# First loads over two queues, whole x tiles, a full-height gate matmul, and an order laid out anew

## The chip, the cores and the metric

One core of a Trainium2 chip runs the kernel. The metric is device time in microseconds of one execution. Its engines work beside each other and meet only at semaphores: TensorE (PE, with its weight loads shown as PEld), VectorE (DVE), ScalarE (ACT), GpSimd (POOL) and SyncE (SP), which here only issues DMAs.

## What is computed

The input x is 2048 tokens of 512 numbers in bf16. Two branches work on it, and a gate of one number for each token mixes them:

```python
g = sigmoid((x * gate_w).sum(-1, keepdims=True))
a = A(x)   # 32 heads of 16; 4 segments of 512 tokens: causal softmax inside a segment,
           # plus a linear memory (phi(q) M / phi(q) z) of the segments before; then @ wo
b = B(x)   # h = relu(x @ W_gate) * (x @ W_up), 1792 wide; then h @ W_down
out = g * a + (1 - g) * b
```

The row `gate_w` has 512 numbers. The kernel needs it on all 128 partitions, so that VectorE can multiply a tile of 128 tokens by it and sum along the row.

## The kernel before

**Stages.** The tokens are worked in four segments of 512. For each segment TensorE makes q and k (transposed, line 788) and v (by tokens, line 786) from x transposed, then visits attention 18 times: a visit (line 908, helper `visit`) computes scores of four heads at once, each head in 32 rows of the array. ScalarE takes the exponential of a visit (line 924), GpSimd masks its diagonal (line 930), and TensorE multiplies by v in packed form (line 964). The feed-forward branch runs beside it: gate and up matmuls (line 1038), relu on ScalarE or VectorE (lines 1046, 1047), the product on VectorE (line 1049), and for each segment the down matmuls (line 1077) and the output projection (line 1070) into one bank. The accumulated memory of the keys is line 831, its use line 851.

**The order.** No loop order is fixed. `program` describes every instruction as an `Op` with the engines that can do it, an estimate of its time, what it reads and writes, and a queue with a priority. `Sched.run` then places one op after the other, by the estimated times, on five engines and 16 DMA semaphores, and writes each engine's instruction list with the waits that it needs. Each engine then runs its list strictly in that order. The planner adds `SWITCH` (line 28) where TensorE changes between kinds of matmul, has a DMA land by a formula in `place` (line 405), and a list of seeds (line 546), one for each 8 us of planned time, that shifts priorities and breaks ties (`knob`, `jitter`). Changing one of these can move every later instruction. `after` on an op is the earliest planned time of its start: 6400 ns for the gate row's matmul, 12000 ns for the first visit.

**The start.** Before anything else can run, x must be transposed for segment 0. `load` puts loads on the list of SP or of ACT (line 598). Before, SP issues four x tiles (into `hT`), four tiles of wq, four of wk, four of wv, the small `braw`, then four half-width tiles of W_gate (`wg`), four of W_up (`wu`), and the second halves. ACT issues a tiny load of wq's corner and the gate row (into row 0 of `oTt`); later, between its other work, it issues tiny loads of the corners of W_gate, W_up and W_down, all into `adT`, so that each waits for the one before. TensorE runs filler matmuls on constants (line 670), transposes the x tiles against an identity that GpSimd has built (lines 647, 648; the matmuls are line 683), and DVE and ACT copy the results to `xT` (lines 693, 695). Tiles 0 and 1 are copied whole, tiles 2 and 3 in halves. Then come more filler matmuls (`warm1`, line 701), the first q matmuls, and the matmul that spreads the gate row over the partitions (line 704): its stationary operand is one row of ones, its moving operand row 0 of `oTt`. ACT copies that to `gwb` (line 706) and DVE multiplies and sums (line 734).

In the first part of q, three output tiles take the first, then the second tile of wq, and so on, so that a matmul can start as soon as its tile of wq is there. The copies out of PSUM are lines 793 (ACT) and 797, 801, 814 (DVE). At most two banks are held by projections at a time.

The places in the planner that the change touches:

```python
op.end = self.dma_busy + (1400.0 if start < 16000.0 else 5200.0 if start < 60000.0 else 3200.0)
...
xps.append(pe(lambda e: e.matmul(PL[:, 2, :], lhsT=nc.const_aps.tensor(1.0, [128, 128], BF16)[0:1, :], rhs=V.oTt[0:1, :], start=True, stop=True), 300, reads=["oTt"], writes=["bankL2"], name="gwx"))
```

Of the kernel before, what the change touches and what calls it, by code (L numbers as in the profile page):

```python
# [11 lines left out]
BF16 = mybir.dt.bfloat16  # L12
# [12 lines left out]
TNN = 4  # L25
STRICT = 6000.0
PE_LAT = 175.0
SWITCH = 100.0
GATE_T = {1: 44000.0, 2: 90000.0, 3: 140000.0}
UNIT_T = 400.0  # L30
NBLK = 36
# [91 lines left out]
class Sched:  # L123
# [240 lines left out]
    def place(self, op, e, start):  # L364
        op.eng = e
        if op.ep is not None and op.role == "w" and op.ep.bank is None:
            got = self._banks(op, e)[0]
            for ep, bi in zip([g[0] for g in got], sorted(g[1] for g in got) if op.ep.cls == "main" else [g[1] for g in got]):
                for i in range(bi, bi + ep.nb):
                    if self.bank_ep[i] is not None:  # L370
                        op.preds += [(r, False) for r in self.bank_ep[i].readers]
                    self.bank_ep[i] = ep
                ep.bank = bi
        if e == "pool" and self.yield_to is not None:
            op.preds.append((self.yield_to, False))
# [12 lines left out]
        if e == "pool":  # L388
            if start > self.now["pool"] + 1.0:
                self.pool_from = start  # L390
        if e == "pe":
            if op.mode != self.mode or start > self.now[e] + 60.0:
                occ += SWITCH
            self.mode = op.mode
        if op.dma:
            d = min(range(self.ndma), key=lambda i: (self.dma_end.get(i, 0.0), i))
            st = f"dma{d}"
            if self.cnt[st] > 0:
                self._waits(e, {st: self.cnt[st]})
            self.cnt[st] += 1  # L400
            self.semval[st, self.cnt[st]] = self.semval.get((st, self.cnt[st] - 1), 0) + 16 * op.nd
            inc = 16
            issued = start + occ
            self.dma_busy = max(self.dma_busy, issued) + op.nbytes / 340.0
            op.end = self.dma_busy + (1400.0 if start < 16000.0 else 5200.0 if start < 60000.0 else 3200.0)
            self.dma_end[d] = op.end
        else:
            st = e
            self.cnt[st] += 1
            inc = 1  # L410
            op.end = start + occ + op.lat
        idx = self.cnt[st]
        self.prog[e].append(("ins", op, st, inc))
        op.stream, op.idx, op.start, op.done = st, idx, start, True
        if op.mates:
            self.mates = op.mates
        if e == "pe" and op.ep is not None and op.ep.cls == "main":
            self.low_from = True
        sn = dict(self.know[e])
        sn[st] = max(sn[st], idx)  # L420
        self.snap[st][idx] = sn
        self.now[e] = start + occ
        self.busy[e] += occ
        self.log.append((start, start + occ, e, op.name))
# [115 lines left out]
def build_kernel(nc, A_x, A_wq, A_wk, A_wv, A_wo, A_beta, W_g, W_u, W_d, gate_w, out):  # L540
    _, S, D = A_x.shape
    F = W_g.shape[1]
    assert D == 512 and S % 512 == 0 and F % 128 == 0
    NSEG, KT, NF, NT = S // 512, D // 128, F // 128, S // 128
    EPS, SCALE = 1e-6, 16 ** -0.5
    sc = Sched(seeds=(140892, 575458, 0, 581332, 635069, 619273, 262375, 763595, 0, 238677, 585783, 19046, 187739, 0, 462444, 519459, 197962, 296149, 243870, 832001, 511906, 535245, 636171, 100007, 0, 121574, 418075, 0, 0, 346384, 0,))
    T = {}
    with contextlib.ExitStack() as stack:
        for name, shape, dt in plan(S, D, F):
            T[name] = stack.enter_context(nc.sbuf_tensor(name, shape, dt))  # L550
        PS = stack.enter_context(nc.psum_tensor("ps", [128, 8, 512], F32))
        for st in sc.streams:
            sc.sem[st] = stack.enter_context(nc.semaphore(f"s_{st}"))
        program(sc, nc, T, PS, A_x, A_wq, A_wk, A_wv, A_wo, A_beta, W_g, W_u, W_d, gate_w, out, NSEG, KT, NF, NT, EPS, SCALE)
        with nc.Block() as block:
            sc.emit(block)
    return sc


def program(sc, nc, T, PS, A_x, A_wq, A_wk, A_wv, A_wo, A_beta, W_g, W_u, W_d, gate_w, out, NSEG, KT, NF, NT, EPS, SCALE):  # L560
    V = type("V", (), T)
# [28 lines left out]
        return PS[:, ep.bank, :] if ep.nb == 1 else PS[:, ep.bank:ep.bank + 2, :]  # L590

    def xt(c):
        return [f"xT{c % XR}_{kt}" for kt in range(KT)] if c % XR else [f"xT0_{i}" for i in (range(6) if c == 0 else (0, 1, 2, 4))]

    lact, lsp = [], []

    def load(eng, names, dst, src, nbytes, occ=460.0):
        (lact if eng == "act" else lsp).append(dma(eng, lambda e, dst=dst, src=src: e.dma_start(dst, src), nbytes, occ=occ, writes=names, name="ld" + names[0]))  # L598
    x0 = A_x[0, 0:512, :].rearrange("(i p) d -> p i d", p=128)
    def touch(n, src):  # L600
        load("act", ["adT"], V.adT[0:16, 32 * n:32 * n + 32], src, 1024)
    touch(0, A_wq[0:16, 0:32])
    load("act", ["oTt"], V.oTt[0:1, :], gate_w.rearrange("(a n) -> a n", a=1), 1024)
    for i in range(4):
        load("sp", [f"hT{i}"], V.hT[:, i, :], x0[:, i, :], 1 << 17)
    for nm, w, src in (("wq", V.wq, A_wq), ("wk", V.wk, A_wk), ("wv", V.wv, A_wv)):
        for kt in range(KT):
            load("sp", [f"{nm}{kt}"], w[:, kt, :], src[kt * 128:(kt + 1) * 128, :], 1 << 17)
    half = (NF // 2) * 128
    hs_ = ((0, half), (half, NF * 128))  # L610

# [50 lines left out]
        ds.append(dve(lambda e, b=b: e.memset(PS[:, 4 + b, :], 0.0), 500, writes=[f"init{b}"], name=f"init{b}"))  # L662
    ds.append(dve(lambda e: e.reduce_sum(V.pm[:, :], V.pm8[:, :].rearrange("q (j p) -> q p j", p=2), AX.X), 180, reads=["pm8"], writes=["pm"], name="pm"))
    sc.queue(0, ds)
    sc.queue(1, st)

    def warm(m, n, k, b):
        def fn(e):
# [3 lines left out]
        return pe(fn, m * n * (0.834 if k == 0 else 0.5), writes=[f"bankL{b}"], name=f"warm{k}")  # L672

    xps, xcs = [warm(5, 512, 0, 3)], []
    for n, (i, k0, k1, bank, eng) in enumerate(((0, 0, 4, 0, "dve"), (1, 0, 4, 1, "act"), (2, 0, 2, 2, "dve"), (2, 2, 4, None, "act"), (3, 0, 2, 3, "dve"), (3, 2, 4, None, "act"))):
        ep = Epoch("att") if bank is None else None

        def B(ep=ep, bank=bank):
            return A(ep) if bank is None else PL[:, bank, :]

        def fx(e, i=i, k0=k0, k1=k1, B=B):
            for kt in range(k0, k1):
                ins = e.matmul(B()[:, kt * 128:(kt + 1) * 128], lhsT=V.hT[:, i, kt * 128:(kt + 1) * 128], rhs=V.ident[:], start=True, stop=True)  # L683
            return ins
        w = 128 * (k1 - k0)
        bk = [] if bank is None else [f"bankL{bank}"]
        xps.append(pe(fx, 108 * (k1 - k0), reads=[f"hT{i}", "ident"], writes=bk, name=f"xt{n}", ep=ep, role=None if ep is None else "w"))

        def src(B=B, k0=k0, k1=k1):
            return B()[:, k0 * 128:k1 * 128].rearrange("q (k t) -> q k t", t=128)  # L690
        dst = V.xT[:, k0:k1, i * 128:(i + 1) * 128]
        if eng == "dve":
            xcs.append(dve(lambda e, d=dst, src=src: e.tensor_copy(d, src()), t_dve(w), reads=bk, writes=[f"xT0_{n}"], name=f"xc{n}", ep=ep, role=None if ep is None else "r"))
        else:
            xcs.append(act(lambda e, d=dst, src=src: e.activation(d, src(), ACT.Copy), t_act(w), reads=bk, writes=[f"xT0_{n}"], name=f"xc{n}", ep=ep, role=None if ep is None else "r"))
# [1 line left out]
    epw = Epoch("att")  # L697

    def warm1(e):
        for n in (128, 128, 128, 128):  # L700
            ins = e.matmul(A(epw)[:, 0:n], lhsT=nc.const_aps.tensor(1.0, [128, 128], BF16), rhs=nc.const_aps.tensor(1.0, [128, n], BF16), start=True, stop=True)
        return ins
    xps.append(pe(warm1, 380, name="warm1", ep=epw, role="w"))
    xps.append(pe(lambda e: e.matmul(PL[:, 2, :], lhsT=nc.const_aps.tensor(1.0, [128, 128], BF16)[0:1, :], rhs=V.oTt[0:1, :], start=True, stop=True), 300, reads=["oTt"], writes=["bankL2"], name="gwx"))  # L704
    xps[-1].after = 6400.0
    xcs.append(act(lambda e: e.activation(V.gwb[:], PL[:, 2, :], ACT.Copy), t_act(512), reads=["bankL2"], writes=["gwb"], name="gwc"))
    sc.queue(0, xps)
# [66 lines left out]
    def proj(s):  # L774
# [3 lines left out]
        def pj(w, col, name, wname, tokmajor=False):  # L778
# [3 lines left out]
            for k0 in range(0, KT, step):  # L782
                def fn(e, k0=k0):
# [3 lines left out]
                        else:  # L787
                            ins = e.matmul(A(ep)[:, :], lhsT=w[:, kt, col * 128:(col + 1) * 128], rhs=V.xT[:, kt, tok:tok + 512], start=(kt == 0), stop=(kt == KT - 1))  # L788
                    return ins
                pes.append(pe(fn, mm(512, step), reads=[f"{wname}{kt}" for kt in range(k0, k0 + step)] + (xt(s) if not early or k0 > 1 else [x for x in xt(s) if x not in ("xT0_3", "xT0_5")]), name=f"{name}{s}_{col}", ep=ep, role="w2" if k0 else "w"))  # L790
            return ep
        def cp(fn, **k):
            return sc.add(Op([("dve", lambda e: fn(e, e.tensor_copy), t_dve(512)), ("act", lambda e: fn(e, lambda d, x: e.activation(d, x, ACT.Copy)), t_act(512))], **k))
# [404 lines left out]
```

## Time and profile before

| what | us |
|---|---|
| median of 3 runs | 264.85 |
| lowest, highest | 264.82, 264.95 |
| the profiled execution | 265.14 |
| its span, first to last instruction | 263.4 |
| TensorE busy | 255.4 |
| ACT busy | 184.9 |
| DVE busy | 181.0 |
| POOL busy | 129.8 |

The span is the time between the first and the last instruction in the trace; the execution's own time is 1.7 us more. The view of the waits gives for each engine and line how long it sat idle and what ended that. The order of time lists instructions merged into runs of the same kind: start, length from first start to last end, engine, line, operation, operands and count. A run's length holds the drain of its last matmul, so starts are compared with starts. A DMA's line is that of its issue; its landing is told by the view of its tile. The table by stretches has for each engine the busy time and count, then TensorE's granted clock, the DMA share and GB/s.

### The profile page before, as it was taken

Reading aid. Unit: us, or ns where it says so; the run is one execution under the profiler, and the core shown is the slowest. Engines: PE = TensorE matmul, PEld = TensorE weight load, DVE = VectorE, ACT = ScalarE, POOL = GpSimd, SP = SyncE. Lnnn points to the kernel's source line nnn. Section 1 sums busy time; section 2 is a strip of 40 time slices with the busy share of each in tenths; the row PEclk is TensorE's granted clock in tenths of the full one; section 3 lists DMA queues with packets and bytes.
Section 4 is the critical chain, followed back from the end, with each engine's and each line's share of the span. In section 5 each row is a group of like instructions: output and inputs, shape, how many; then the busy total and the mean of one; then the engine's idle time right before and its main releaser. Section 6 shows DMA issues by size and latency. Waiting matters only on the chain.

```text
span 263.4 us, 6630 instructions
## 1 busy us (share of the span) xinstructions
PE 255.4 (97%) x2713; PEld 113.6 (43%) x2748; DVE 181.0 (69%) x355; ACT 184.9 (70%) x159; POOL 129.8 (49%) x295
## 2 busy tenths in 40 slices
PE   8999999999999999999999999999999999999996
PEld 4444444444343544434343444444444444444444
DVE  5788788889788555787877765775873857267610
ACT  4577589976788956877778986978765765767021
POOL 3025646564646354774646366776564443535200
PEclk9999999999999999999999999999999999999999
DMA  6899584024250023210273014110032101100011
GB/s 182 235 383 223 85 270 132 4 41 71 56 115 27 3 65 80 63 41 3 58 138 74 20 42 81 41 25 20 20 80 49 22 0 42 41 2 0 2 40 40
DMA packets 34527, 19.22 MB, mean 73 GB/s; under 512 B 24001, under 2 KB 33986, under 8 KB 34498
## 3 DMA queue, kind: packets, MB, share of 16 engines
q1 hardware_dynamic: 34368, 18.80, 29.4%
q8 instruction: 21, 0.34, 0.5%
q14 instruction: 8, 0.07, 0.1%
q10 hardware_dynamic: 130, 0.01, 0.0%
HBM read 9.75 MB, written 2.11 MB: 45 GB/s over the span
## 4 chain that ended last, share of the span: by engine, by line
PE 94%; DMA 2%; issue 2%; SPq 0%; DVE 0%; DVEq 0%
PE ps L1038 36%; PE ps L1077 19%; PE ps L788 11%; PE ps L908 9%; PE ps L964 7%; PE ps L1070 5%; PE ps L786 5%; DMA phik<-ek 1%; PE ps L851 1%; DMA hT<-in_A_x_dram 1%; PE ps L831 1%; SPq L598 0%; PE ps L683 0%; DVE osb L1086 0%; PE ps L704 0%
## 5 line engine op out<-in xcount | busy, mean ns | idle before, releaser
L930 POOL TENSOR_SCALAR_AFFINE_SELECT E<-E 64x256 bf16<-64x256 bf16 (+1 forms) x256 | 108.9, 437 | 110.1 <-ACT E L924 81.3
L924 ACT ACTIVATE E<-ps 128x2048 bf16<-128x2048 f32 x72 | 135.1, 1876 | 36.4 <-PE ps L908 36.0
L1038 PE MATMUL ps<-xT,wu 128*128 128x512 bf16 x214 | 57.5, 380 | 1.4 <-issue 1.3
L1038 PE MATMUL ps<-xT,wg 128*128 128x512 bf16 x217 | 57.7, 380 | 0.8 <-issue 0.6
L1077 PE MATMUL ps<-wd,hT 128*128 128x512 bf16 (+2 forms) x229 | 52.3, 366 | 1.1 <-issue 1.0
L1049 DVE TENSOR_TENSOR hT<-ps,rl 128x512 bf16<-128x512 f32 x56 | 38.2, 682 | 18.8 <-PE ps L1038 18.4
L974 DVE STREAM_TRANSPOSE Tn<-ps 128x512 f32<-128x512 f32 x32 | 21.2, 695 | 17.8 <-PE ps L964 17.7
L1038 PEld LDWEIGHTS ps<-xT,wg 128*128 128x128 bf16 x224 | 20.6, 98 | 25.9 <-issue 3.5
L1077 PEld LDWEIGHTS ps<-wd,hT 128*128 128x128 bf16 x238 | 21.4, 98 | 23.8 <-issue 2.8
L1038 PEld LDWEIGHTS ps<-xT,wu 128*128 128x128 bf16 x224 | 19.9, 98 | 25.7 <-issue 3.2
L908 PE MATMUL ps<-qT,kp 32*128 32x192 bf16 (+7 forms) x512 | 28.6, 287 | 0.0
L1047 DVE TENSOR_SCALAR rl<-ps 128x512 bf16<-128x512 f32 x31 | 21.3, 688 | 5.0 <-PE ps L1038 4.3
L1046 ACT ACTIVATE rl<-ps 128x512 bf16<-128x512 f32 x25 | 14.9, 598 | 12.8 <-PE ps L1038 12.8
L908 PEld LDWEIGHTS ps<-qT,kp 32*128 32x128 bf16 x512 | 8.2, 92 | 25.8 <-issue 14.4
L964 PE MATMUL ps<-E,vaug 64*17 64x128 bf16 (+7 forms) x512 | 18.7, 283 | 0.0
L964 PE MATMUL ps<-E,vsh 64*17 64x128 bf16 (+7 forms) x512 | 18.3, 283 | 0.0
L1087 ACT ACTIVATE osb<-ps,omg 128x512 bf16<-128x512 f32 (+1 forms) x9 | 6.1, 675 | 15.6 <-PE ps L1070 14.4
L1086 DVE TENSOR_SCALAR osb<-ps,omg 128x512 bf16<-128x512 f32 (+1 forms) x8 | 5.6, 700 | 16.3 <-PE ps L1070 10.1
L1070 PE MATMUL ps<-wo,oT 128*128 128x512 bf16 (+2 forms) x68 | 16.5, 367 | 0.0
L788 PE MATMUL ps<-xT,wk 128*128 128x512 bf16 x62 | 16.2, 380 | 0.2 <-issue 0.2
L788 PE MATMUL ps<-xT,wq 128*128 128x512 bf16 x62 | 15.9, 379 | 0.3 <-issue 0.2
L786 PE MATMUL ps<-wv,xT 128*128 128x512 bf16 x59 | 15.1, 380 | 0.7 <-issue 0.6
(74 smaller groups left out, 232.7 us busy)
## 6 DMA issues: line engine op xcount, KB each, us to landing
vsh<-vaug SPq DMA_DIRECT2D x8, 272.0 KB, 3.9
out_dram<-osb SPq DMA_DIRECT2D x15, 128.0 KB, 1.7
wg<-in_B_W_gate_dram SPq DMA_DIRECT2D x8, 224.0 KB, 5.1
wu<-in_B_W_up_dram SPq DMA_DIRECT2D x8, 224.0 KB, 5.3
wd<-in_B_W_down_dram SPq DMA_DIRECT2D x1, 1792.0 KB, 9.1
osb<-in_A_x_dram SPq DMA_DIRECT2D x12, 128.0 KB, 2.3
hT<-in_A_x_dram SPq DMA_DIRECT2D x4, 128.0 KB, 2.3
wq<-in_A_wq_dram SPq DMA_DIRECT2D x4, 128.0 KB, 2.9
```

The source lines that it names most:

```text
L786: ins = e.matmul(A(ep)[:, :], lhsT=V.xT[:, kt, tok + col * 128:tok + (col + 1) * 128], rhs=w[:, kt, :], start=(kt == 0), stop=(kt == KT - 1))
L788: ins = e.matmul(A(ep)[:, :], lhsT=w[:, kt, col * 128:(col + 1) * 128], rhs=V.xT[:, kt, tok:tok + 512], start=(kt == 0), stop=(kt == KT - 1))
L908: ins = q.matmul(dst, lhsT=V.kp[r, kslot(s, G), c, :], rhs=V.qT[r, qslot(s, G), q0:q0 + w], start=True, stop=True, tile_position=(32 * jj, ...
L924: acts.append(act(lambda a: a.activation(V.E[:, base * 512:base * 512 + min(2048, 4 * W)], PF[:, 0:min(2048, 4 * W)], ACT.Exp, scale=SCALE ...
L930: pools.append(pool(lambda g, ap=ap, lim=lim, pat=pat: g.affine_select(out=ap, in_=ap, compare_op=ALU.is_ge, fill=0.0, base=lim, pattern=[ ...
L964: ins = q.matmul(A(eps[p])[32 * jj:32 * jj + 17, 64 * (c + u):64 * (c + u + n)], lhsT=v[:, 8 * G + 2 * jj + p, :], rhs=V.E[r, f:f + 64 * n ...
L974: ds.append(dve(lambda e, p=p, ep=eps[p]: e.transpose(V.Tn[:, 2 * (G % (TNN // 2)) + p, :], A(ep)[:, :]), t_dve(512), writes=[f"Tn{2 * (G ...
L1038: ins = e.matmul(A(ep)[:, :], lhsT=w[:, kt, f * 128:(f + 1) * 128], rhs=V.xT[:, kt, c % XR * 512:(c % XR + 1) * 512], start=(kt == 0), sto ...
L1047: ("dve", lambda e, ep=eg, r=r: e.tensor_scalar(V.rl[:, r, :], A(ep)[:, :], 0.0, None, ALU.max), t_dve(512))],
L1049: evs.append(dve(lambda e, ep=eu, r=r, hs=hs: e.tensor_tensor(V.hT[:, hs, :], A(ep)[:, :], V.rl[:, r, :], ALU.mult), t_dve(512), reads=[f" ...
L1070: ins = e.matmul(A(ep)[:, 0:c1 - c0], lhsT=V.oT[:, ot[G], i * 128:(i + 1) * 128], rhs=V.wo[:, G, c0:c1], start=st_ and G == 0, stop=sp_ an ...
L1077: ins = e.matmul(A(ep)[:, 0:c1 - c0], lhsT=V.hT[:, slots[f], i * 128:(i + 1) * 128], rhs=V.wd[:, f, c0:c1], start=st_ and f == f0, stop=sp ...
```

## The change

The two small x, wq and gate loads change queue, x tiles are transposed and copied whole, the filler is longer, the gate row's matmul takes all 128 rows (GpSimd first sets `oTt` to zero, so that 127 rows add nothing), and three numbers of the planner and its seeds differ. From line 602 on, the changed kernel's lines are one higher.

```diff
-SWITCH = 100.0
+SWITCH = 104.0
...
-            op.end = self.dma_busy + (1400.0 if start < 16000.0 else 5200.0 if start < 60000.0 else 3200.0)
+            op.end = self.dma_busy + (1100.0 if start < 16000.0 else 5200.0 if start < 60000.0 else 3200.0)
...
-    sc = Sched(seeds=(140892, 575458, 0, 581332, ...))     # 31 seeds
+    sc = Sched(seeds=(140892, 423927, 621999, 605862, ...))  # 33 seeds
...
-    touch(0, A_wq[0:16, 0:32])
-    load("act", ["oTt"], V.oTt[0:1, :], gate_w.rearrange("(a n) -> a n", a=1), 1024)
+    gz = pool(lambda e: e.memset(V.oTt[:, :], 0.0), 250, writes=["oTt"], name="gz")
     for i in range(4):
-        load("sp", [f"hT{i}"], V.hT[:, i, :], x0[:, i, :], 1 << 17)
+        load(("sp", "act")[i % 2], [f"hT{i}"], V.hT[:, i, :], x0[:, i, :], 1 << 17)
     for nm, w, src in (("wq", V.wq, A_wq), ("wk", V.wk, A_wk), ("wv", V.wv, A_wv)):
         for kt in range(KT):
-            load("sp", [f"{nm}{kt}"], w[:, kt, :], src[kt * 128:(kt + 1) * 128, :], 1 << 17)
+            load("act" if nm == "wq" and kt == 1 else "sp", [f"{nm}{kt}"], w[:, kt, :], src[kt * 128:(kt + 1) * 128, :], 1 << 17)
+        if nm == "wq":
+            load("sp", ["oTt"], V.oTt[0:1, :], gate_w.rearrange("(a n) -> a n", a=1), 1024)
...
-    sc.queue(1, st)
+    sc.queue(1, [st[0], gz] + st[1:])
...
-    for n, (i, k0, k1, bank, eng) in enumerate(((0, 0, 4, 0, "dve"), (1, 0, 4, 1, "act"), (2, 0, 2, 2, "dve"), (2, 2, 4, None, "act"), (3, 0, 2, 3, "dve"), (3, 2, 4, None, "act"))):
+    for n, (i, k0, k1, bank, eng) in enumerate(((0, 0, 4, 0, "dve"), (1, 0, 4, 1, "act"), (2, 0, 4, 2, "dve"), (3, 0, 4, 3, "act"))):
...
-        for n in (128, 128, 128, 128):
+        for n in (512, 512, 512, 128):
...
-    xps.append(pe(lambda e: e.matmul(PL[:, 2, :], lhsT=nc.const_aps.tensor(1.0, [128, 128], BF16)[0:1, :], rhs=V.oTt[0:1, :], start=True, stop=True), 300, reads=["oTt"], writes=["bankL2"], name="gwx"))
+    xps.append(pe(lambda e: e.matmul(PL[:, 2, :], lhsT=nc.const_aps.tensor(1.0, [128, 128], BF16), rhs=V.oTt[:, :], start=True, stop=True), 216, reads=["oTt"], writes=["bankL2"], name="gwx"))
```

Every q matmul now waits for all four x tiles; before, the first two tiles of wq could be used without the second halves of x tiles 2 and 3.

What that makes of the instruction lists: on SP the order is x0, x2, wq0, wq2, wq3, the gate row, four wk, four wv, `braw`, four wg, four wu, and so on; on ACT x1, x3, wq1, then the activation table. TensorE's list begins with the filler, 16 transposes, the longer filler, two wq matmuls, the gate row's, 14 wq, 6 wk, 2 wg, 4 wk, 2 wg, the first visit (4 matmuls), 2 wk, 2 wu, 4 wk, 2 wu, 4 wg, 12 wv. Before it was the filler, 16 transposes, filler, 4 wq, the gate row's, 12 wq, 14 wk, the first visit, 2 wk, 12 wv, a visit, 4 wv, 4 wg, 4 wu. On ACT the tiny load of W_down's corner now stands between the third q copy and the first k copy; before, it stood behind two k copies. The work itself (projections, feed-forward, 72 visits, 16 second products) is the same in both.

More of the change, by code (lines that the diff above doesn't have):

```diff
@@ L545, in build_kernel @@
     EPS, SCALE = 1e-6, 16 ** -0.5
-    sc = Sched(seeds=(140892, 575458, 0, 581332, 635069, 619273, 262375, 763595, 0, 238677, 585783, 19046, 187739, 0, 462444, 519459, 197962, 296149, 243870, 832001, 511906, 535245, 636171, 100007, 0, 121574, 418075, 0, 0, 346384, 0,))
+    sc = Sched(seeds=(140892, 423927, 621999, 605862, 856097, 597983, 0, 820269, 619327, 0, 896081, 257284, 643444, 61269, 537966, 0, 819204, 36136, 990326, 0, 596070, 54089, 235513, 913573, 135504, 649865, 99322, 0, 0, 0, 975897, 119585, 0,))
     T = {}
@@ L592, in xt @@
     def xt(c):
-        return [f"xT{c % XR}_{kt}" for kt in range(KT)] if c % XR else [f"xT0_{i}" for i in (range(6) if c == 0 else (0, 1, 2, 4))]
+        return [f"xT{c % XR}_{kt}" for kt in range(KT)] if c % XR else [f"xT0_{i}" for i in range(4)]
     lact, lsp = [], []
@@ L699, in warm1 @@
     def warm1(e):
-        for n in (128, 128, 128, 128):
+        for n in (512, 512, 512, 128):
             ins = e.matmul(A(epw)[:, 0:n], lhsT=nc.const_aps.tensor(1.0, [128, 128], BF16), rhs=nc.const_aps.tensor(1.0, [128, n], BF16), start=True, stop=True)
         return ins
-    xps.append(pe(warm1, 380, name="warm1", ep=epw, role="w"))
-    xps.append(pe(lambda e: e.matmul(PL[:, 2, :], lhsT=nc.const_aps.tensor(1.0, [128, 128], BF16)[0:1, :], rhs=V.oTt[0:1, :], start=True, stop=True), 300, reads=["oTt"], writes=["bankL2"], name="gwx"))
+    xps.append(pe(warm1, 760, name="warm1", ep=epw, role="w"))
+    xps.append(pe(lambda e: e.matmul(PL[:, 2, :], lhsT=nc.const_aps.tensor(1.0, [128, 128], BF16), rhs=V.oTt[:, :], start=True, stop=True), 216, reads=["oTt"], writes=["bankL2"], name="gwx"))
     xps[-1].after = 6400.0
@@ L789, in fn @@
                     return ins
-                pes.append(pe(fn, mm(512, step), reads=[f"{wname}{kt}" for kt in range(k0, k0 + step)] + (xt(s) if not early or k0 > 1 else [x for x in xt(s) if x not in ("xT0_3", "xT0_5")]), name=f"{name}{s}_{col}", ep=ep, role="w2" if k0 else "w"))
+                pes.append(pe(fn, mm(512, step), reads=[f"{wname}{kt}" for kt in range(k0, k0 + step)] + xt(s), name=f"{name}{s}_{col}", ep=ep, role="w2" if k0 else "w"))
             return ep
```

## The prediction

> **What bounds the kernel now.** I read the busy shares, then the chain of waits, then TensorE's idle times, then the first 20 us in order of time.
>
> From the page, the busy shares and the chain that ended last:
> ```profile
> PE 255.4 (97%) x2713; PEld 113.6 (43%) x2748; DVE 181.0 (69%) x355; ACT 184.9 (70%) x159; POOL 129.8 (49%) x295
> ...
> PE 94%; DMA 2%; issue 2%; SPq 0%; DVE 0%; DVEq 0%
> ```
> TensorE is busy 97% and carries 94% of the chain; no other engine is above 70%. Its weight loads in the view of the waits (total us, times, longest us):
> ```profile
> PEld ps L908 <- issue: 14.4, 34, 0.4
> PEld ps L1038 <- issue: 6.7, 31, 0.2
> ...
> PEld ps L683 <- DMA hT<-in_A_x_dram: 1.6, 4, 0.7
> ```
> The only waits above 0.5 us come before 3 us (the start and the x tiles). All others are the 0.2 or 0.4 us of a change between whole-array matmuls and the packed ones of attention (L908, L964), also where another engine is named. So behind the start this kernel never waits for data. The end is the first projection's start, plus a fixed sum of matmuls, plus the changes of mode, plus a tail of some 2.5 us. Whatever makes TensorE wait is therefore paid in full.
>
> The start, TensorE alone in order of time (start us, length us):
> ```profile
> 2.93 2.55 PE L683 MATMUL ps<-ident,hT 128*128 128x128 bf16 x16
> 5.28 0.50 PE L701 MATMUL ps<-const-bfloat16-1.0 128*128 128x128 bf16 x4
> 5.88 1.02 PE L788 MATMUL ps<-xT,wq 128*128 128x512 bf16 x4
> 6.83 0.38 PE L704 MATMUL ps<-oTt,const-bfloat16-1.0 1*128 1x512 bf16 x1
> 7.15 2.76 PE L788 MATMUL ps<-xT,wq 128*128 128x512 bf16 x12
> 9.75 3.19 PE L788 MATMUL ps<-xT,wk 128*128 128x512 bf16 x13
> ```
> Twelve matmuls take 2.76, one alone 0.38, so each adds (2.76 - 0.38)/11 = 0.216 us: the slot that I count with. The first wq starts at 5.88 and all runs on from there.
>
> **The change, part by part.**
>
> *First loads over two queues.* The SP queue issues one load each 0.47 us (the four of x in 1.81, four of wk from 4.56 to 6.42). x tiles 1 and 3 and wq1 move to ACT's queue, the gate row moves to SP's behind wq3, and one small ACT load is gone. On SP each load behind wq3 has two fewer ahead of it (three gone, one added): 0.95 us earlier. ACT issues three loads for two, some 0.45 us more ahead of its table load (1.81 to 3.09), which would then end near 3.6; its first copy began at 4.13 and still finds it done. What comes earlier are the x tiles: the last landed at 2.19 + 2.6 = 4.8 and its transposes began at 4.87. But the DMA engines were not idle:
> ```profile
> 2.00:4.00 2.00, 2.00 (x11) 0.86 (x9) 1.45 (x5) 1.09 (x1) 1.07 (x5) 1.00 0.84 247
> 4.00:6.00 2.00, 1.72 (x14) 1.20 (x14) 1.14 (x3) 1.36 (x3) 0.00 (x0) 1.00 0.91 259
> ...
> 10.00:12.00 2.00, 1.95 (x10) 0.94 (x10) 1.80 (x6) 0.92 (x2) 0.00 (x0) 1.00 0.80 160
> ```
> In this table by stretches the last two columns are the DMA share and GB/s: 84 to 91% with 247 to 259 GB/s. Four tiles of 131 KB at that rate need 2.0 us from about 1.9, so the last lands at 4.0 to 4.4, not earlier by the full 0.95. [...]
>
> *Whole copies, longer filler.* Before, tiles 2 and 3 were copied in halves of 0.42 (DVE) and 0.38 (ACT). Whole copies are 0.69 on DVE and about 0.6 on ACT (x0 and x2; x1 and x3). With x3's transposes over at 4.7 to 5.1 (4 slots of 0.107 and 0.2 of drain), its copy ends at 5.3 to 5.7 and 0.12 later wq may start: the old pair of copies ended at 5.90, and wq's first start was 5.88. Meanwhile the filler grows from 512 to 1664 columns. The five 512-wide fillers at the start (L670) are 0.427 apart (0.84 to 2.51), twice the 0.216 of later, and the transposes 0.107. The array turns fast at about 5.5. The filler from 4.5 or 4.7 runs two matmuls slow and the rest fast: over at 5.6 to 5.75. First wq at about 5.7: **-0.15 us** (bounds -0.4, both early; +0.15, the filler wholly slow to 6.0).
>
> *Gate row with 128 rows.* The one-row matmul sits between wq's: the fourth wq starts at 5.88 + 1.02 - 0.38 = 6.52, the next at 7.15, so 0.63 - 0.22 = 0.41 us are spent on one slot; half is the change of array mode and back. With 128 rows it is one more matmul in the row: 0.22. **-0.2 us** (bounds 0 and -0.2). The new memset on POOL (128x512) stands ahead of the identity's select, which was over at 1.37; the nearest memsets there took 0.20, so even at 0.8 us it hides behind x0's landing at 2.9.
>
> *Order.* The built program has the same 946 whole-array matmuls of the main work, 72 attention visits and 16 second products. The breaks of packed work in the whole-array stream fall from 74 to 73. A visit such as that at 12.87 costs 13.19 - 12.56 - 0.22 = 0.42 for 0.22 of work, so a break is 0.2; the one saved joins others: **-0.15 us** (0 to -0.2).
>
> *What the new order asks of the loads.* Before, wk's and wv's matmuls came first and wg was first used at 17.5. Now, after 16 wq, the gate row and 6 wk, TensorE is to use wg's first two tiles, then after 4 more wk the next two, then one visit, 2 wk, and wu's first two. It reaches the first wg at 5.7 + 23 x 0.216 = 10.7 and the second pair at 10.7 + 6 x 0.216 = 12.0. SP's issues before, in order of time:
> ```profile
> 8.83 1.85 SPq L598 DMA_DIRECT2D wg<-in_B_W_gate_dram  x4
> 10.73 1.85 SPq L598 DMA_DIRECT2D wu<-in_B_W_up_dram  x4
> ```
> and the time from issue to landing over all wg loads, from the view of that tile:
> ```profile
> DMA to landing us min/median/max: 4.1/5.1/5.6
> ```
> One by one the first four wg took 4.1, 4.2, 4.7 and 4.8 us from issue: 12.95, 13.5, 14.5 and 15.0. Issued 0.95 earlier they land at 12.0, 12.6, 13.5 and 14.1; a fuller start takes off perhaps 0.2 more, since the loads ahead of them then queue sooner. TensorE waits from 10.7 to 12.4 for the second tile, runs six matmuls to 13.7, and waits to 13.9 for the fourth. Then the visit, two wk: it is at wu's first pair at 13.9 + 0.43 + 0.42 + 0.43 = 15.2 against 16.2 - 1.15 = 15.1, and at the next pair at 16.5 against 16.3: in time. The wait is thus the fourth tile's landing less the time at which it would be reached: 13.9 - 12.0 = **+1.9 us**. Bounds: 3.0 if landings do not move (15.0), and 0 if the low stretch from 10 to 12 us (160 GB/s with loads queued) were filled at the 386 GB/s of 14 to 16 us. Nothing else can run meanwhile, since wk and wv stand behind wg in TensorE's own order, though their data is there.
>
> ACT gets a wait too: the small load from W_down now stands ahead of its first kT copy, and waits for that from W_up to land. That one is issued near 8.3 and took 2.9 (8.88 to 11.7): 11.2, then 0.33 of issue and 0.60 of copy, so kT at 12.1. The third wk group needs that bank and is due at 10.7 + 4 x 0.216 = 11.6. It hides behind the wait for wg; without that it costs 0.6.
>
> *Sum.* -0.15 - 0.2 - 0.15 + 1.9 = **+1.4 us**. The profiled execution took 265.14 with a span of 263.4: 266.5 expected for it. The median of the runs is 264.85, 0.29 below: 264.85 + 1.4 = **266.25**.
>
> **Rivals.**
> 1. *The loads arrive in time, the kernel is faster.* If two queues fill the DMA engines from 2 us on and the stretch of 160 GB/s closes, wg's fourth tile lands by 12.0. It decides at that point: each 0.1 us later costs 0.1. ACT's wait must shrink too. Then -0.4 - 0.2 - 0.15 = -0.75: 264.1. For it: 3.0 MB up to that tile would need only 7.9 us at 386 GB/s from 1.9. Against: with the 128 KB tiles no stretch of 2 us shows more than 268 (6 to 8 us). Chance 0.10.
> 2. *Only ACT's wait is left.* wg is near in time, kT at 12.1 holds the third wk group 0.6: 264.85 - 0.5 + 0.6 = 264.95, no change. Chance 0.14.
> 3. *Landings hardly move, or a second wait comes later in the new order.* 3.0 for 1.9, or one more wait of 1 us, such as a transpose by DMA late for segment 1: 267.4 or more. Against: the old order never waited behind the start. Chance 0.10.
> 4. *The filler stays slow.* [...] By the rows, if the step came 1 us later, some three slots would cost 0.2 more each: +0.6, of which the wait for wg takes all. Without that wait the result is case 2's time; it is counted there.
>
> **How the numbers follow.** Forecast (wait of 1 to 2.5 us, 265.4 to 266.9): 0.66; rivals 0.10, 0.14, 0.10. About 0.2% (0.53 us) is what a measurement of this kernel can tell from no change: faster means under 264.3. Faster 0.10; same 0.16 (case 2 and the forecast's lower edge); slower 0.74. The range 264.9 to 267.4 leaves out case 1 and half of case 3, and the lower edge of case 2.
>
> **What would show it.** Right: TensorE idle before the first wg matmuls, 1 us or more, ended by a DMA, near 10.7 and again near 13.5; L705 without idle time around it; first wq near 5.7. Wrong: wg tiles landing by 11 to 12 us; idle time on TensorE above 0.5 us anywhere behind 17 us, which would be an order that is worse of itself; a first wq at 6 or later.

## The result and the profile after

The changed kernel takes 267.89 us (median of 4 runs, 267.85 to 268.48) against 264.84 for the kernel before in the same comparison (4 runs, 264.78 to 264.95): a ratio of 1.012, 95% interval 1.0102 to 1.0137. It is slower by 3.05 us; 1.4 were forecast. The profiled execution took 267.89 with a span of 265.9, before 265.14 and 263.4. TensorE's last matmul starts 2.56 us later than before (263.27 for 260.71), so these 2.56 us are what is accounted for below. Of the 2.75 between the two profiled executions the other 0.2 lies outside the spans.

The page's busy shares and the chain that ended last:
```profile
PE 256.0 (96%) x2715; PEld 114.1 (43%) x2748; DVE 181.6 (68%) x354; ACT 184.8 (70%) x158; POOL 129.3 (49%) x296
...
PE 92%; DMA 4%; issue 2%; DVE 1%; ACT 0%; ACTq 0%; DVEq 0%
```
TensorE's busy time is 0.6 higher, its share of the chain 2% lower, DMA's 2% higher: time went into waiting for loads. Its weight loads in the view of the waits (total us, times, longest us):
```profile
PEld ps L909 <- issue: 13.6, 32, 0.4
PEld ps L1039 <- issue: 9.0, 30, 2.0
...
PEld ps L684 <- DMA hT<-in_A_x_dram: 1.2, 1, 1.2
```
The longest wait at the gate and up matmuls (L1039, before L1038) was 0.2 and is 2.0. TensorE in order of time (start, length):
```profile
3.38 1.89 PE L684 MATMUL ps<-ident,hT 128*128 128x128 bf16 x16 [0.25 <-DMA hT<-in_A_x_dram]
5.06 1.59 PE L702 MATMUL ps<-const-bfloat16-1.0 128*128 128x512 bf16 x4
6.45 0.74 PE L789 MATMUL ps<-xT,wq 128*128 128x512 bf16 x2
7.03 0.38 PE L705 MATMUL ps<-oTt,const-bfloat16-1.0 128*128 128x512 bf16 x1
7.24 3.19 PE L789 MATMUL ps<-xT,wq 128*128 128x512 bf16 x14
10.26 1.46 PE L789 MATMUL ps<-xT,wk 128*128 128x512 bf16 x6
13.27 0.38 PE L1039 MATMUL ps<-xT,wg 128*128 128x512 bf16 x1 [1.55 <-ACT kT L794]
13.70 1.02 PE L789 MATMUL ps<-xT,wk 128*128 128x512 bf16 x4
14.56 0.59 PE L1039 MATMUL ps<-xT,wg 128*128 128x512 bf16 x2
```
The first wq starts at 6.45 (5.88 before), and the fillers at L702 are 0.427 apart to the end: half clock until 6.74, where the trace's record of the granted clock steps to full (5.50 before). The column of the clock in the tables by stretches shows 1.00 ahead of the step too, since the record begins with it; the half pace is read from the starts, 0.427 apart and then 0.216. The gate row's matmul lies in the row of wq at one slot (7.03 to 7.24). The sixth wk starts at 11.34; the next slot would be at 11.56, and the first wg starts at 13.27: 1.71 us of wait. The releaser named is the kT copy. That is a coincidence of 0.1 us: the wg tiles land at 12.55, 13.13, 13.74 and 14.31, the matmuls of a pair need the second, and its weight load starts at 13.24. The second pair, at 14.56, waits for nothing.

The loads, by SP's issues, by the view of the tile, and by stretches (last two columns DMA share and GB/s):
```profile
7.71 1.86 SPq L598 DMA_DIRECT2D wg<-in_B_W_gate_dram  x4
9.61 2.08 SPq L598 DMA_DIRECT2D wu<-in_B_W_up_dram  x4
```
```profile
DMA to landing us min/median/max: 4.8/5.4/5.9
```
```profile
2.00:4.00 2.00, 1.75 (x10) 0.77 (x9) 1.04 (x4) 1.28 (x1) 1.41 (x7) 1.00 0.97 298
4.00:6.00 2.00, 2.00 (x15) 1.45 (x14) 1.38 (x2) 1.19 (x2) 0.00 (x0) 1.00 0.95 290
6.00:8.00 2.00, 2.00 (x10) 0.91 (x9) 0.00 (x0) 0.56 (x1) 0.00 (x0) 1.00 0.94 301
8.00:10.00 2.00, 2.00 (x11) 0.88 (x9) 1.93 (x6) 0.87 (x3) 0.00 (x0) 1.00 0.76 201
10.00:12.00 2.00, 1.72 (x8) 0.59 (x6) 1.29 (x5) 0.85 (x2) 0.00 (x0) 1.00 0.90 243
```
The stretch in which wg's load begins, before:
```profile
8.00:10.00 2.00, 2.00 (x11) 0.92 (x10) 1.85 (x6) 1.09 (x2) 0.00 (x0) 1.00 0.86 240
```
The wg tiles are issued 1.12 us earlier than before and land 0.4 to 0.7 earlier: each takes 0.4 to 0.7 longer. From 2 to 6 us the DMA engines were 0.84 to 0.91 busy and are 0.95 to 0.97. But while wg itself moves, from 8 to 12 us, they are 0.76 and 0.90 busy, where they were 0.86 and 0.80, so full engines alone do not explain it. The trace marks 16 parts of each load as they land. Of the second wg tile half are there by 11.87, the last at 13.13; before, by 12.99 and 13.53. The middle moved by the 1.12 of the issue, the last part by 0.40 only. Why the last part lags is not shown.

A second wait stands behind 17 us, where the forecast had none:
```profile
42.17 0.60 PE L1039 MATMUL ps<-xT,wu 128*128 128x512 bf16 x2
43.24 0.61 PE L1039 MATMUL ps<-xT,wu 128*128 128x512 bf16 x2 [0.47 <-issue]
```
Two wu matmuls, 0.63 us of nothing, two more of the same product. No semaphore is waited for. In the view of DMAs for 40.7 to 42 us a second queue appears:
```profile
q1 hardware_dynamic: 439, 0.44, 103.0%
q8 instruction: 1, 0.02, 5.5%
```
That is read as TensorE's instructions coming in: packets of 16384 bytes, 21 in the run for 5513 records of TensorE, one for some 260. The second begins at 40.73 and is over at 41.87, in the middle of the load of W_down (1.8 MB, issued 33.95, landed 44.12). Counted over all of TensorE's records in the trace (matmuls, weight loads and its 50 for semaphores and drains), it stops ahead of the 702nd, a weight load whose matmul is the 703rd, in every kernel below that stops there.

The 2.56 us: start +0.57, and +0.15 for one wq matmul still at half clock; gate row -0.20; one break less and a wait of 0.14 near 110 us that only before has, -0.28; first wg +1.71; near 42 us +0.63. Sum 2.58.

### The profile page after: what moved, and what is told of

It reads as the page before. It is cut to its first block, busy times and chain, and to the rows that moved or that the text cites. A ratio compares the mean times of both kernels' runs of the same rounds, so it can differ in the third digit from the quotient of the medians.

```text
span 265.9 us, 6626 instructions
## 1 busy us (share of the span) xinstructions
PE 256.0 (96%) x2715; PEld 114.1 (43%) x2748; DVE 181.6 (68%) x354; ACT 184.8 (70%) x158; POOL 129.3 (49%) x296
## 4 chain that ended last, share of the span: by engine, by line
PE 92%; DMA 4%; issue 2%; DVE 1%; ACT 0%; ACTq 0%; DVEq 0%
PE ps L1039 37%; PE ps L1078 18%; PE ps L909 9%; PE ps L789 9%; PE ps L965 6%; PE ps L1071 5%; PE ps L787 5%; DMA adT<-in_B_W_up_dram 1%; PE ps L852 1%; DMA adT<-in_B_W_gate_dram 1%; DMA hT<-in_A_x_dram 1%; PE ps L684 1%; PE ps L832 1%; DVE rl L1048 0%; ACT kT L794 0%
## 5 line engine op out<-in xcount | busy, mean ns | idle before, releaser
L1039 PE MATMUL ps<-xT,wg 128*128 128x512 bf16 x216 | 57.2, 380 | 2.4 <-ACT kT L794 1.5
L1039 PE MATMUL ps<-xT,wu 128*128 128x512 bf16 x217 | 57.8, 380 | 1.5 <-issue 1.3
L1050 DVE TENSOR_TENSOR hT<-ps,rl 128x512 bf16<-128x512 f32 x56 | 38.2, 682 | 15.6 <-PE ps L1039 14.9
L1039 PEld LDWEIGHTS ps<-xT,wg 128*128 128x128 bf16 x224 | 20.4, 98 | 27.7 <-issue 5.4
L1039 PEld LDWEIGHTS ps<-xT,wu 128*128 128x128 bf16 x224 | 20.1, 98 | 26.4 <-issue 3.5
L975 DVE STREAM_TRANSPOSE Tn<-ps 128x512 f32<-128x512 f32 x32 | 21.2, 696 | 13.6 <-PE ps L965 13.5
L1048 DVE TENSOR_SCALAR rl<-ps 128x512 bf16<-128x512 f32 x33 | 22.7, 688 | 7.5 <-PE ps L1039 6.5
L1047 ACT ACTIVATE rl<-ps 128x512 bf16<-128x512 f32 x23 | 13.7, 597 | 11.9 <-PE ps L1039 11.9
L1087 DVE TENSOR_SCALAR osb<-ps,omg 128x512 bf16<-128x512 f32 (+1 forms) x9 | 6.3, 702 | 16.8 <-PE ps L1071 10.5
L1088 ACT ACTIVATE osb<-ps,omg 128x512 bf16<-128x512 f32 (+1 forms) x8 | 5.4, 674 | 17.0 <-PE ps L1071 14.0
L789 PE MATMUL ps<-xT,wq 128*128 128x512 bf16 x63 | 16.6, 382 | 0.0
```

The lines of the kernel that those rows point to most:

```text
L975: ds.append(dve(lambda e, p=p, ep=eps[p]: e.transpose(V.Tn[:, 2 * (G % (TNN // 2)) + p, :], A(ep)[:, :]), t_dve(512), writes=[f"Tn{2 * (G ...
L1039: ins = e.matmul(A(ep)[:, :], lhsT=w[:, kt, f * 128:(f + 1) * 128], rhs=V.xT[:, kt, c % XR * 512:(c % XR + 1) * 512], start=(kt == 0), sto ...
L1048: ("dve", lambda e, ep=eg, r=r: e.tensor_scalar(V.rl[:, r, :], A(ep)[:, :], 0.0, None, ALU.max), t_dve(512))],
L1050: evs.append(dve(lambda e, ep=eu, r=r, hs=hs: e.tensor_tensor(V.hT[:, hs, :], A(ep)[:, :], V.rl[:, r, :], ALU.mult), t_dve(512), reads=[f" ...
```

## The experiments

My theory was that sum: start, wg's landing, and instructions that come late behind W_down's load. Rivals: ACT's wait for W_up's corner is what holds TensorE; the order is slow of itself; the second wait has another cause. In the kernels below each engine's order is written out as a fixed list, so that an edit moves only what it names.

**wg ahead of wv on SP.**
```diff
 SP: ... 4 wk,
-    4 wv, braw, 4 wg, 4 wu
+    4 wg, 4 wv, braw, 4 wu
```


> The changed kernel with its instruction lists fixed as they are, but SP issues wg's four first tiles ahead of wv's four (1.9 us earlier). Theory: TensorE's wait of 1.7 us at the first wg matmuls ends with the landing of wg's second tile (13.13). It should then land near 11.3 and that wait should be gone; ACT's first kT copy, which stands behind the small load that waits for the W_up corner (12.2), then holds the third wk group to about 13.3, due at 12.4: some 0.9 us of the 1.7 come back there. Time 267.0, between 266.6 and 267.3. Rival: the wait ends with ACT's kT copy (13.27), as the profile's line names it, and the time stays at 267.9.

Measured 268.53, ratio 1.0123 [1.0101, 1.0144]. A miss. The wg tiles land by 11.88 and that wait is gone, but another takes its place. ACT, then TensorE:
```profile
13.45 0.37 ACTq L598 DMA_DIRECT2D adT<-in_B_W_down_dram  x1
13.86 0.60 ACT L794 ACTIVATE kT<-ps 128x512 bf16<-128x512 f32 x1 [2.38 <-PE ps L789]
```
```profile
15.17 0.39 PE L909 MATMUL ps<-qT,kp 32*128 32x512 bf16 x4 [1.29 <-DVE kp L806]
```
W_up's corner lands at 13.43; only then may ACT issue W_down's corner and copy kT, and the first visit stands behind that. The wait near 42 is 1.2 here.

**The same, and the corners free of one another.**
```diff
-        load("act", ["adT"], V.adT[0:16, 32 * n:32 * n + 32], src, 1024)
+        load("act", [f"adT_{n}"], V.adT[0:16, 32 * n:32 * n + 32], src, 1024)
```


> As the one before, and the four small corner loads no longer wait for each other, so that ACT's kT copy waits for nothing but TensorE. Theory: two causes hide each other, the landing of wg and ACT's wait; with both gone nothing holds TensorE until 17 us, and 1.7 us are gained: 266.2 (265.9 to 266.5). Rival: the DMA engines are simply full, and another load (wv) is late instead: 267 or more.

Measured 267.22, ratio 1.0087 [1.0066, 1.0109]: 1.3 better than the last, 1.0 worse than expected. ACT's wait is gone; 0.57 is waited for wu at 14.4 (the second tile landed at 14.8) and 0.86 near 42.

**The same, and the short filler.**
```diff
-        for n in (512, 512, 512, 128):
+        for n in (128, 128, 128, 128):
```


> As the one before, with the filler ahead of the first q matmuls cut back to 4 x 128 columns. Theory: the filler, wholly at half clock, ends 0.45 us behind the last x copy (5.91) and holds the first wq; without it wq starts at 6.0, but at half clock until the step near 6.7, so 0.2 to 0.4 us are gained: 265.9. Rival (the clock decides): wq runs slow for as long as the filler did, and nothing is gained, 266.2; or the step comes later, and it is slower.

Measured 267.57, ratio 1.0094 [1.0077, 1.0112]: no gain. The first wq starts at 5.90 (6.55), and TensorE waits the longer for wu:
```profile
15.03 0.59 PE L1039 MATMUL ps<-xT,wu 128*128 128x512 bf16 x2 [1.40 <-DMA wu<-in_B_W_up_dram]
```
What the start gains, the loads take: start and wait are not two terms.

**The changed kernel with the short filler alone.** (The diff of the last, made to the changed kernel.)

> The changed kernel with the short filler of before alone. First query matmul near 5.9 to 6.0 instead of 6.45. My theory: the landings of the first gate weights do not depend on TensorE, so TensorE reaches them 0.5 earlier and waits 0.5 longer: 267.9 (267.4 to 268.3), wait 2.2 to 2.4. Rival (the start and the wait add up): 267.35 with an unchanged wait of 1.7.

Measured 269.06 (267.5 to 270.2), ratio 1.0142 [1.01, 1.0184]; the rival's 267.35 is out.
```profile
6.14 0.61 PE L789 MATMUL ps<-xT,wq 128*128 128x512 bf16 x2 [0.41 <-ACT xT L696]
...
13.65 0.38 PE L1039 MATMUL ps<-xT,wg 128*128 128x512 bf16 x1 [2.27 <-DMA wg<-in_B_W_gate_dram]
```
The start is 0.31 earlier, the wait 2.43 instead of 1.71, and now the load itself is named. The wait came as expected, the time did not: 267.9 was expected, 268.3 at most. The second wg tile landed later (13.51), 1.18 is waited near 42, and 0.41 at 97. The longest of the runs, 270.17, also had a granted clock of 0.994 for 1.000.

**The changed kernel with ACT's corners free alone.** (The diff of the second kernel, made to the changed kernel.)

> The changed kernel with one thing undone: ACT's small corner loads from W_gate, W_up and W_down no longer wait for one another, so ACT's first kT copy is free of the landing of W_up's corner. My theory: TensorE waits for the first gate weights (landings 12.5 to 14.3), and ACT's wait only ends at the same time: time stays at 267.9 (267.4 to 268.3), TensorE's wait at 11.3 stays at 1.7 to 2.2. Rival (what the profile names as releaser, the kT copy, is the cause): the wait shrinks to about 0.3 and the time to 266.4.

Measured 268.14 (267.2 to 268.46), ratio 1.0116 [1.0095, 1.0136]. The rival's 266.4 is out. The profiled execution was the fastest of the four and waits only 0.78 at wg:
```profile
12.41 0.38 PE L1039 MATMUL ps<-xT,wg 128*128 128x512 bf16 x1 [0.62 <-ACT omg L747]
```
Again ACT is named, and again the second wg tile decides: here it landed at 12.27. Over five kernels of this order the first wg starts 0.13 or 0.14 behind that landing: 13.13 and 13.27 (the changed kernel), 12.27 and 12.41, 13.51 and 13.65, 13.74 and 13.87, 13.07 and 13.21. The landing moves by 1.5 us between these executions.

**W_down's load later** (issued at 58.8, landed 66.4).
```diff
-SP: ... wo, W_down, x for the gate, 2 transposes, x for the gate, ...
+SP: ... wo, x for the gate, 2 transposes, x for the gate, W_down, ...
```


> The changed kernel as it is, with the one load of W_down (1.8 MB) issued near 58 us instead of 34. Theory: TensorE's idle 0.6 us at 42.4, for which no semaphore is awaited, is its own instruction fetch (16 KB, begun at 40.7, some 170 instructions late) standing behind W_down's load. The fetch should then begin near 36 and the idle time be gone: 267.25. Rival: that time belongs to something else in the order (PSUM banks, DVE), and stays: 267.9.

Measured 269.16, ratio 1.0146 [1.0122, 1.0169], but the wait near 42 is gone:
```profile
42.77 1.04 PE L1039 MATMUL ps<-xT,wu 128*128 128x512 bf16 x4
```
The fetch begins at 38.53 instead of 40.73, not at 36 as expected. The total missed the expected 267.25. In the profiled execution (267.97, granted clock 1.000) the second wg tile landed at 13.74, a wait of 2.17, and there is a new 0.33 at 96. The other three runs (269.07 to 269.34) had a granted clock of 0.993 to 0.994. Over 267 us a clock lower by 0.006 to 0.007 is worth an estimated 1.6 to 1.9 us, so the median of 269.16 holds that too. Why their clock was lower is not shown.

**W_down's load doubled.**
```diff
+    wd2 = nc.dram_tensor("wd2", [NF * 128, 512], BF16).ap()
+    load("sp", ["wd2"], wd2.rearrange("(f p) n -> p f n", p=128), W_d.rearrange("(f p) n -> p f n", p=128), NF * 128 * 1024)
     load("sp", ["wd"], V.wd[:], W_d.rearrange("(f p) n -> p f n", p=128), NF * 128 * 1024)
```
The second load stands behind the first on SP's list.

> The changed kernel with W_down's load of 1.8 MB followed by a second one of the same size (into DRAM, read by nobody). My theory: TensorE's second instruction fetch stands behind both, begins near 50 instead of 40.7, and TensorE runs dry at the same place, near 42.4, for 8 to 10 us instead of 0.63: 275 to 278. Rival (the wait of 0.63 has another cause than the fetch behind that load, a semaphore or the mode change): no wait over 1 us near 42, 267.5 to 268.5.

Measured 269.25 (one run, before 264.95). Both missed: the wait near 42 is 1.28, not 8 to 10, and not gone.
```profile
42.33 0.61 PE L1041 MATMUL ps<-xT,wu 128*128 128x512 bf16 x2
44.05 0.61 PE L1041 MATMUL ps<-xT,wu 128*128 128x512 bf16 x2 [1.11 <-issue]
```
So the fetch does not stand behind the whole load. The traces show this instead (us; the 500th and 703rd are counted over all of TensorE's records):

| kernel | 500th starts | fetch begins | over | 703rd could start | does start |
|---|---|---|---|---|---|
| before | 33.2 | 33.7 | 35.0 | 42.4 | 42.4 |
| changed | 37.6 | 40.7 | 41.9 | 42.6 | 43.24 |
| short filler alone | 38.2 | 41.7 | 42.9 | 43.2 | 44.37 |
| W_down doubled | 37.8 | 41.6 | 42.8 | 42.8 | 44.05 |
| W_down later | 38.2 | 38.5 | 39.7 | 43.2 | 43.2 |

A fetch begins about when the 500th record starts; it comes 0.3 to 0.5 later in the two rows without W_down's packets ahead of it and 3.1 to 3.8 later while these fill the engines (their queue's share is 110.2% from 37.7 to 40.7 in the changed kernel, 109.8% from 38 to 41.6 with W_down doubled), with one load waiting or two. (In the next two kernels, with wo's load and x in flight instead, it is 1.0 and 1.9 late, and nothing stops.) Its packet takes 1.1 to 1.3, and TensorE goes on 1.3 to 1.5 after its end. That makes 5.6 to 6.3 with the load, and TensorE needs 5.0 from the 500th to the 703rd. In the old order it takes 9.2. What differs is this group, in the changed kernel and in the kernel before:
```profile
38.12 0.66 PE L832 MATMUL ps<-vaug,phik 128*32 128x34 bf16 x64
```
```profile
42.05 0.66 PE L831 MATMUL ps<-vaug,phik 128*32 128x34 bf16 x64
```
64 small matmuls with 64 weight loads, 128 instructions in 0.66 us: the new order runs them right behind the request and has 5 us of instructions left; the old one makes q and k first. Both seem needed for the wait: W_down in flight, and the short instructions early. The load's part was tried; moving the 64 matmuls alone was not. The 0.24 to 0.44 near 93 to 97 us in some kernels looks the same: always at the 1974th record, 1.2 to 1.5 behind a fetch.

**Three waits taken away.** TensorE runs the first 12 wv matmuls ahead of the first wg, the corners are free, W_down is late.
```diff
-TensorE: ... 6 wk, 2 wg, 4 wk, 2 wg, visit, 2 wk, 2 wu, 4 wk, 2 wu, 4 wg, 12 wv
+TensorE: ... 10 wk, visit, 6 wk, 12 wv, 4 wg, 4 wu, visit, ...
```


> The changed kernel with its three waits taken away and the order otherwise as the change has it: the twelve matmuls of the value weights come ahead of the first gate and up weights on TensorE, the corner touches of ACT do not wait for one another, and W_down's load is issued at the visit where it no longer stands ahead of TensorE's instruction fetch. If the order as such is no worse than before, what is left is the start +0.57, the gate row -0.2 and one break less -0.14: 265.1 to 265.3. If the new order has a cost of its own that the waits do not show, 266 or more. A wait of a few tenths for an up weight near 14 us would show in the trace as TensorE idle there and is to be counted apart.

Measured 266.77, ratio 1.0053 [1.0032, 1.0073]. The trace still shows three waits: 0.27 near 14, 0.24 at 95 (the fetch), and one of my own making, for the bank of a v copy that DVE does late:
```profile
22.76 1.04 PE L1039 MATMUL ps<-xT,wg 128*128 128x512 bf16 x4 [0.86 <-DVE vaug L815]
```
From slot to start that is 1.02 (the idle time shown begins when the matmul before has drained). Without the three it is 265.24, as expected, but only by subtraction. So the next kernel repairs it.

**The same, banks and the v copy mended, short filler.**
```diff
-DVE: ... vone, relu, ek, v copy, product
+DVE: ... v copy, relu, vone, ek, product
```


> The changed kernel with value weights first on TensorE, corners free, W_down late, as before, and now also the PSUM bank that TensorE waited for at 21.5 in that kernel (1.0 us, a value copy placed late by my own edit) freed earlier, and the short filler of before. If the order itself costs nothing once nothing waits in it: start +0.05, gate row -0.2, one break less -0.15, and the 0.25 at 95 us that both kernels with a late W_down showed: 264.8 (264.5 to 265.1). If the new order has a cost that shows in no wait: 265.6 or more.

Measured 265.09, ratio 1.0016 [0.9994, 1.0038]: the time of before. Both 264.8 and the rival's 265.6 lie in the interval, so the trace must decide. Its last matmul starts 0.22 earlier than that of before. The start gives -0.46 (first wq at 5.42, clock step at 3.94), the gate row -0.20, its load, which lands late for so early a start, +0.36, and the fetch at 93 us +0.24: -0.06. What is left for the order is -0.16. It contains a wait of 0.11 ahead of the first visit; without that it is -0.27, which is the break saved and the wait near 110 that is gone (-0.28 in the changed kernel). So in this execution the new order costs nothing that does not show as a wait. It is one execution; of its ten runs two took 266.85 and 267.16.

**The old order with the whole new start.**
```diff
 SP, ACT, transposes, copies, filler, gate row: as in the change
-order behind the start: new
+order behind the start: old
```


> The order and every load of before behind the start, with the whole start of the change: loads split over SP and ACT, x tiles transposed and copied whole, long filler, gate row with 128 rows. My theory (three terms: start +0.57, wait for the first gate weights +1.7, wait of 0.63 near 42 us for TensorE's own instructions; gate row -0.2, one break less -0.14): only the start and the gate row are left, so first query matmul at about 6.45, no wait at the first gate weights, none near 42 us, and 264.85 + 0.57 - 0.2 = 265.2. Rival a (the order itself costs more than its waits show, so the start is worth nothing): 264.7. Rival b (the split loads delay the value weights or later ones too, and the wait comes back in the old order): over 266.

Measured 265.21 against 265.21, ratio 0.9994 [0.9971, 1.0017]; 264.56 to 266.06 over 12 runs.
```profile
5.22 1.25 PE L702 MATMUL ps<-const-bfloat16-1.0 128*128 128x512 bf16 x4
6.31 1.02 PE L789 MATMUL ps<-xT,wq 128*128 128x512 bf16 x4
```
In its profile the start costs 0.43 and the gate row gives 0.2 back. Expected was 0.35 more than before; the runs say -0.16, interval -0.77 to +0.45. The expected 0.35 lies inside that interval, so what the start costs over many executions is not decided. The clock step came at 5.98 here and at 6.74 in the changed kernel, so part of the 0.57 may belong to that one execution. Rival b is out: in the old order no wait comes back.

**The split of the loads alone.**
```diff
-load("sp", [f"hT{i}"], ...)
+load(("sp", "act")[i % 2], [f"hT{i}"], ...)
```
(wq1 and the gate row as in the change.)

> The kernel before with one thing changed: the first loads split over SP and ACT (half-tile transposes, short filler and the gate row as before). If the split alone is what moves the start later, x0 lands near 3.3 instead of 2.88 and the first query matmul comes 0.3 to 0.5 later than 5.88: 265.2 to 265.4. If the long filler and the whole-tile copies are what does it (my guess, two thirds), the first query matmul stays within 0.15 of 5.88 and the time is 264.8 to 265.0. If the split helps, as x3 lands earlier (4.3 instead of 4.83): 264.5.

Measured 265.32 against 265.21, ratio 0.9994 [0.997, 1.0017]: no difference, as guessed.
```profile
5.89 1.02 PE L788 MATMUL ps<-xT,wq 128*128 128x512 bf16 x4 [0.37 <-ACT xT L695]
```
x0 lands at 3.63 instead of 2.88, x3 at 4.52 instead of 4.83, and the first wq starts where it did (5.88). That points to the whole copies and the long filler at half clock for the 0.57. But the clock step came at 4.86 here and at 6.74 in the changed kernel, so what the split costs with a late step is not shown.

**The gate row with 128 rows alone.**
```diff
+    gz = pool(lambda e: e.memset(V.oTt[:, :], 0.0), 250, writes=["oTt"], name="gz")
-... lhsT=nc.const_aps.tensor(1.0, [128, 128], BF16)[0:1, :], rhs=V.oTt[0:1, :] ...
+... lhsT=nc.const_aps.tensor(1.0, [128, 128], BF16), rhs=V.oTt[:, :] ...
```


> The kernel before with the gate row's matmul of 128 rows alone; nothing else moved. By the sum, 0.41 becomes 0.22 at that one matmul and nothing waits on it: 264.65, that is 0.2 faster than before. Rival: the memset of the tall operand on GpSimd ahead of the identity delays the transposes, and the gain is lost at the start: 264.85 to 265.2.

Measured 264.80 (11 runs, 264.50 to 265.06) against 265.21, ratio 0.9972 [0.995, 0.9995].
```profile
5.72 1.02 PE L789 MATMUL ps<-xT,wq 128*128 128x512 bf16 x4 [0.28 <-ACT xT L696]
6.58 0.38 PE L705 MATMUL ps<-oTt,const-bfloat16-1.0 128*128 128x512 bf16 x1
6.80 0.38 PE L789 MATMUL ps<-xT,wq 128*128 128x512 bf16 x1
```
6.58 is four slots behind 5.72, 6.80 one more: the one-row matmul's extra 0.2 is gone. Expected was 0.2 less than before; the runs say 0.1 to 1.3 less. The profiled execution's start is also 0.16 earlier, with a clock step at 3.55 for 5.50; that the edit has no part in that step is not shown. Of the kernels run this has the lowest median. The gain is small: four of the 35 runs of before in this comparison lie at 267.2 to 267.3 and widen the interval, and in the other comparisons before had medians of 264.84 to 264.99, 0.05 to 0.2 above 264.80.

## Why the prediction was wrong

The sign and the main mechanism were right, the size was not: 267.89 lies 0.5 above the range. By its own steps:

- **What bounds the kernel.** Right: all that TensorE waits is paid. "Never waits for data" holds but for the 0.14 near 110.
- **First wq, -0.15.** Wrong: +0.57, and 0.15 at half clock behind it. Three assumptions failed. The last x tile landed in the range given (4.29), but x0 came 0.45 later than before (3.33), so the 16 slow transposes ended late and the filler began at 5.06, not at 4.5 to 4.7. The clock step was taken as fixed at 5.5. It is not: in 14 traces it lies between 3.55 and 7.42. And so the filler ran wholly slow, 3 x 0.427 + 0.107 = 1.39, to 6.45; the bound for that case had the too early begin.
- **Why that step cost nothing in the end.** Rival 4 said that a later start is taken up by the wait for wg, and it is: with an early step at 4.78 (W_down doubled) the first wq is at 5.94 and the wait 2.29; in the changed kernel 6.45 and 1.71. TensorE leaves this place when the second wg tile has landed. Start and wait should have been one term.
- **The wait for wg, +1.9.** Measured 1.71, which looks right and is not, since it began 0.86 later than the forecast's 10.7. The failing sentence is "issued 0.95 earlier they land at 12.0, 12.6, 13.5 and 14.1": it let landings follow issues. They were issued 1.12 earlier and landed at 12.55, 13.13, 13.74 and 14.31. With the second at 13.13 the second pair starts at 14.56, where the forecast had 13.9: **0.66 us too early**. The prediction set the landings of the x tiles by the DMA share and rate that the trace of before shows (0.84 to 0.91, 247 to 259 GB/s), and did not do so for wg behind them. From 2 to 6 us the share became 0.95 to 0.97; while wg moved it was 0.76 and 0.90, so the share alone does not tell its landing either. That wg's landing did not follow its issue is measured; why is open.
- **ACT's wait.** Right in place, 1.2 too early: the corner landed at 12.23 for a forecast of 11.2, the kT copy ended at 13.27 for 12.1. It is hidden, as said; without wg's wait it costs more than the 0.6 given, 1.36 in the first experiment, since W_up's corner then landed at 13.43.
- **No wait behind 17 us.** Wrong, by **0.63**: TensorE's own instructions. Rival 3 allowed for a second wait, but not for this one, and at 1 us.
- **Gate row -0.2 and order -0.15.** -0.20, and -0.14 for the break; the wait near 110 that went gives another 0.14.

From the forecast's 1.4: +0.66 for the landing, +0.63 for the instructions, -0.14 near 110: 2.55, for 2.56 measured. The remaining 0.3 between 2.75 (profiled executions) and 3.05 (medians) is that the profiled execution of before was 0.3 above its median.

## What to carry to other kernels

Where the engine waits for a load, its own start before that is no separate term: find the landing, and count from there. A landing need not follow its issue: here the issue moved 1.12 and the landings 0.4 to 0.7, so take the landing of the last part from a trace, or give it that range. And read the instruction queue's row beside the others: an engine that stops in the middle of one product, with no semaphore and "issue" as the releaser, may be waiting for its own instructions.

## What the runs showed of the hardware that was not expected

- TensorE stops with no semaphore waited for: 0.63 to 1.28 us at one place, 0.24 to 0.44 at another, always at the same two records (the 703rd and the 1974th), 1.2 to 1.5 us behind a packet of 16384 bytes on the queue that the profile names `instruction`. That its instructions come late is read from this, and from the 21 such packets in the run, one for some 260 records. At the first place it stops when a 1.8 MB load is in flight and 128 short instructions run in 0.66 us right behind the request; with that load later it does not. That the short instructions are needed for it is argued from the old order, not tried alone.
- How much load is queued behind hardly matters for that fetch: 3.1 us late behind one W_down, 3.8 behind two, 3.5 behind one again in the kernel with the short filler.
- The clock step lies between 3.55 and 7.42 us after the first instruction in the 14 traces, in kernels that differ little up to there: a spread of 3.9, and no fixed delay. What sets it is not shown. The full clock then lasts 259.41 us in the kernel before and in the changed one alike.
- The x loads of 131 KB, over two queues, landed the first tile later (x0 at 3.2 to 3.6 for 2.88) and the last earlier (4.2 to 4.5 for 4.83).
- The second wg tile's landing moves by 1.5 us between executions of one order. The runs of the new order spread by 0.6 to 2.7 us in their comparisons, those of before by 0.2 in the first and by 0.5, 1.0 and 2.6 in others. Whether the landing makes that spread is not shown, with one trace for each kernel.
